# First batch of an agent-attention and gated-FFN kernel: loads and conversions reordered ahead of the first up product, and one cast placed behind an output copy

## The chip, the cores and the metric

The kernel runs on one core of a Trainium2 chip. The metric is the device time of one execution in microseconds (us), lower is better; runs are given by their median. The engines are named as in the profile: PE (TensorE matmuls), PEld (its weight loads), DVE (VectorE), ACT (ScalarE), POOL (GpSimd) and SP (SyncE, which issues most DMAs).

## What is computed

```python
# per batch b of 4; N = 12480 tokens, C = 128, 49 agents
def sm(a, b):
    s = scale * (a @ b.transpose(0, 2, 1)); e = np.exp(s - s.max(-1, keepdims=True))
    return e / (e.sum(-1, keepdims=True) + 1e-09)
agent_v = sm(agents, k) @ v          # over all keys of the batch
x = sm(q, agents) @ agent_v          # each query token
h = x @ w_in                         # 128 -> 2048
out = (h * sigmoid(1.702 * h)) @ w_out   # 2048 -> 128
```

Weights come as 64-bit floats and are converted on DVE.

## The kernel before, in words

The agents' values of a batch are folded into `w_in`, so that the query softmax feeds an up product of 49 rows with 2048 columns directly (`wh`, `wl` are high and low part of that folded weight). Work runs in **gaps**, one per 128 columns of the hidden layer (`f`, 16 of them) of a group of 960 query tokens (`n`, 52 groups), plus one more gap per group. A gap issues the jobs that a table `at` puts there, an up product with its two activations on ACT (`up`), a high part (`high`: a DMA cast for even `f` and for 1 and 9, else a cast on ACT), a low part on DVE (`low`, three gaps later) and two half down products (`down`, six gaps later). In the last gap of a group `store` copies the two output banks `po[0]` (ACT) and `po[1]` (DVE) to `o`; the next group's first down product writes the same two banks. Within the gaps each engine runs the instructions in the order in which the code writes them.

Ahead of the gaps stands a start phase for batch 0, whose order on each engine a scheduler makes. Its steps:

- 13 key blocks `kt0` land, `first_key_scores` multiplies each with the agents on PE, ACT copies the scores to `score`, DVE keeps a running maximum (`running_max`, L277).
- `key_max` (L285 to L302) reduces it to `max_b`; `key_shift` (L317) subtracts it and `key_exp` (L321) takes the exponentials.
- 13 value blocks `vt0` land in tiles that later hold `wh` and `wl`; 104 products (L657) sum them into `acc_ps`. Value blocks 8 to 12 reuse the tiles of blocks 0 to 5.
- `load_words` loads a quarter of `w_in` or `w_out` (512 KB); `to_float32` converts it with eight DVE instructions (L123 to L135), for `up_weights` into `w_in_sb`, for `down_weights` into `wo_h` and `wo_l`. The words share three buffers.
- `weights_0`, `weights_1` and `weights_parts` turn `acc_ps` into `avT` and fold it into `w_in_sb` (L383), which gives `wh` (ACT, L386) and `wl` (DVE, L387).

Of the conversions only the first of `w_in` stands before the values; the others come behind them, in this code:

Of the kernel before, what the change touches and what calls it, by code (L numbers as in the profile page):

```python
# [8 lines left out]
F32 = mybir.dt.float32  # L9
# [10 lines left out]
KB = 8  # L20
# [10 lines left out]
P_AT = 8  # L31
K_AT = (4, 10, 13)
V_AT = (6, 10)
FIRST_WORDS = 1
FIRST_UP = 2
BY_DMA = (1, 9)
EPS = 1e-09

# [2 lines left out]
def kernel(  # L41
# [273 lines left out]
    def key_shift(g, sub):  # L315
        sc = score[:TB, g * KB : (g + 1) * KB, :]
        sub(out=sc, in0=sc, in1=max_b[:TB].unsqueeze(1).broadcast_to([TB, KB, A]), op=ALU.subtract)  # L317

    def key_exp(g, n):
        sc = score[:TB, g * KB : (g + n) * KB, :]  # L320
        nc.scalar.activation(out=sc, in_=sc, func=AF.Exp, scale=scale)  # L321
# [35 lines left out]
    def weights_0(acc, w):  # L357
# [2 lines left out]
        nc.vector.tensor_add(out=zc, in0=z[0], in1=z[1])  # L360
        w["acc"], w["zc"] = acc, zc

    def weights_1(w):
        ps = two_banks()[:, 0]
        parts = [w["acc"][:, c, i * C : (i + 1) * C] for c in range(2) for i in range(2)]
        for i, part in enumerate(parts):
            nc.tensor.matmul(out=ps[:, 0:P], lhsT=part, rhs=sel, start=(i == 0), stop=(i == len(parts) - 1))
        nc.tensor.matmul(out=ps[:, P : 2 * P], lhsT=w["zc"], rhs=sel, start=True, stop=True)
        rz = work.tile([P, P], F32, name="rz", bufs=1)
        nc.vector.tensor_scalar_add(out=rz, in0=ps[:, P : 2 * P], scalar1=EPS)  # L370
        nc.vector.reciprocal(out=rz, in_=rz)
        avT = work.tile([P, P], F32, name="avT", bufs=1)
        nc.vector.tensor_mul(out=avT, in0=ps[:, 0:P], in1=rz)
        w["avT"] = avT

    def weights_parts(b, w, c):
        if c == 0:
            wts[b] = wpool.tile([P, F], F32R, name="wh"), wpool.tile([P, F], F32R, name="wl")
        wh, wl = wts[b]
        pw = two_banks()  # L380
        for i in range(2):
            s = slice((c + i) * 512, (c + i + 1) * 512)
            nc.tensor.matmul(out=pw[:, i], lhsT=w["avT"], rhs=w_in_sb[:, s], start=True, stop=True)  # L383
        for i in range(2):
            s = slice((c + i) * 512, (c + i + 1) * 512)
            nc.scalar.copy(out=wh[:, s], in_=pw[:, i])  # L386
            nc.vector.tensor_sub(out=wl[:, s], in0=pw[:, i], in1=wh[:, s].bitcast(F32))  # L387

# [166 lines left out]
    def do_query_load(n):  # L555
        if n < B * NG:
            qts[n] = query_load(*divmod(n, NG))
# [56 lines left out]
    def first_keys():  # L614
        tags = [("g", G_BUFS), ("gh", GH_BUFS), ("gl", GL_BUFS)]
        tiles = []
        for tag, bufs in tags:
            tiles += [gpool.tile([P, KB, TB], F32, name="kt0", tag=tag, bufs=bufs) for _ in range(bufs)]
        return tiles[:NKG]

    for g, t in enumerate(first_keys()):
        nc.sync.dma_start(out=t, in_=kT[0, :, g * KB : (g + 1) * KB, :])
        kts[0, g] = t
    do_query_load(0)
    words_in = []
    for g in range(NKG):
        if g % 2 == 0:
            vt0 = wpool.tile([P, 2, KB, C + 1], F32, name="vt0", tag=("wh", "wl")[g // 2 % 2])
            nc.gpsimd.memset(vt0[:, :, :, C :], 1.0)
        vts[0, g] = vt0[:, g % 2]  # L630
        nc.sync.dma_start(out=vt0[:TB, g % 2, :, 0:C], in_=v[0, :, g * KB : (g + 1) * KB, :])
        if g == FIRST_WORDS:
            words_in.append(load_words(w_in, 0))
    words = []
    for i in range(NF // 4):
        if i:
            words_in.append(load_words(w_in, i))
        words.append(load_words(w_out, i))
    for g in range(NKG):
        first_key_scores(g, kts.pop((0, g)))  # L640
    for i in range(4):
        do_query_split(0, i)
    key_max()
    banks[0] = score_banks()
    scores_whole(0, q_parts[0], banks[0][0])
    do_query_load(1)
    do_query_shift(0)
    do_query_exp(0)
    do_query_sums(0)
    do_query_softmax(0)  # L650
    acc_ps = ps_o.tile([P, 512], F32, name="po0")
    for g in range(NKG):
        key_shift(g, nc.vector.tensor_tensor if g == 0 else nc.gpsimd.tensor_tensor)
        key_exp(g, 1)
        vt = vts.pop((0, g))
        for j in range(KB):
            nc.tensor.matmul(  # L657
                out=acc_ps[:A, : C + 1],
                lhsT=score[:TB, g * KB + j, :],
                rhs=vt[:TB, j, :],  # L660
                start=(g == 0 and j == 0),
                stop=(g == NKG - 1 and j == KB - 1),
            )
        if g == FIRST_UP:
            up_weights(0, words_in[0])
        if g == 6:
            do_query_pairs(0)
    accs[0] = work.tile([P, 2, 2 * C + 1], F32, name="acc")
    nc.gpsimd.memset(accs[0], 0.0)
    nc.vector.tensor_copy(out=accs[0][:A, 0, 0:C], in_=acc_ps[:A, 0:C])  # L670
    nc.vector.tensor_copy(out=accs[0][:A, 0, 2 * C :], in_=acc_ps[:A, C : C + 1])
    w0 = {}
    weights_0(accs.pop(0), w0)
    weights_1(w0)
    up_weights(1, words_in[1])
    weights_parts(0, w0, 0)
    down_weights(0, words[0])


    steps = B * NG * NF  # L680
# [37 lines left out]
        take(t + P_AT, 1)  # L718
        put(t + P_AT, lambda m=m: do_query_pairs(m))

    put(0, lambda: up_weights(2, words_in[2]))
    put(1, lambda: down_weights(1, words[1]))
    put(2, lambda: up_weights(3, words_in[3]))
    take(3, 1)
    put(3, lambda: weights_parts(0, w0, 2))
    put(5, lambda: down_weights(2, words[2]))
    put(7, lambda: down_weights(3, words[3]))
    for b in range(B - 1):
        begin = gap_of(b * NG * NF)
        end = gap_of((b + 1) * NG * NF)  # L730
# [47 lines left out]
    po = {}  # L778

    late = []  # L780

    def do_high(u):
        gh[u] = high(u % NF, g[u])

    def do_up(u):
        n, f = divmod(u, NF)
        g[u] = up(f, wts[n // NG], pairs[n])
        if by_dma(f):
            late.append(u)
        else:  # L790
            do_high(u)
        if f == NF - 1:
            pairs.pop(n)

# [14 lines left out]
    def gap(t):  # L809
        n, k = divmod(t - LAG, GAPS)  # L810
        final = n == B * NG - 1
        if t < LAG:
            u = t
        elif final:
            u = n * NF + LAG + k
        elif k == 1:
            u = None
        else:
            u = n * NF + LAG + max(k - 1, 0)
        before, late[:] = list(late), []  # L820
        rest()
        for job in at.pop(t, ()):
            job()
        if u is not None:
            if u < steps:
                do_up(u)
                rest()
            do_low(u - 3)
        if t >= LAG:
            do_downs(n, k)  # L830
        for u in before:
            do_high(u)

    def do_downs(n, k):
        if k == 0:
# [53 lines left out]
```

## Time and profile before

| | |
|---|---|
| runs | 2028.25, 2022.54, 2024.57 us, median 2024.57 |
| profiled execution | 2026.61 us, its span 2024.8 us |
| PE busy | 1953.1 us, 96% of the span |
| DVE, ACT, POOL busy | 77%, 69%, 15% |
| mean granted clock of TensorE | 0.986 |

The 1.8 us between span and time lie outside the profiled instructions. A busy PE is not one at its peak: the ends of matmuls are modelled, and neighbours overlap.

### The profile page before, as it was taken

Reading aid. Unit: us, or ns where it says so; the run is one execution under the profiler, and the core shown is the slowest. Engines: PE = TensorE matmul, PEld = TensorE weight load, DVE = VectorE, ACT = ScalarE, POOL = GpSimd, SP = SyncE. Lnnn points to the kernel's source line nnn. Section 1 sums busy time; section 2 is a strip of 40 time slices with the busy share of each in tenths; the row PEclk is TensorE's granted clock in tenths of the full one; section 3 lists DMA queues with packets and bytes.
Section 4 is the critical chain, followed back from the end, with each engine's and each line's share of the span. In section 5 each row is a group of like instructions: output and inputs, shape, how many; then the busy total and the mean of one; then the engine's idle time right before and its main releaser. Section 6 shows DMA issues by size and latency. Waiting matters only on the chain.

```text
span 2024.8 us, 59521 instructions
## 1 busy us (share of the span) xinstructions
PE 1953.1 (96%) x25158; PEld 1771.6 (87%) x25158; DVE 1553.4 (77%) x2025; ACT 1404.0 (69%) x2407; POOL 303.4 (15%) x642
## 2 busy tenths in 40 slices
PE   8789999999999999999999999999999999999998
PEld 8578998988988989998988889888898998999987
DVE  5687878887878888887867887888886766676765
ACT  3267777767667667677667677777776787777775
POOL 3011111111111111111111111111111111111111
PEclk9689999999999999999999999999999999999999
DMA  9555565666545665656554566566654544545453
GB/s 256 153 166 178 195 186 183 192 192 195 175 160 191 194 191 184 196 181 182 186 167 167 190 203 190 183 186 186 186 172 139 176 170 172 174 171 180 167 177 137
DMA packets 124336, 365.98 MB, mean 181 GB/s; under 512 B 12572, under 2 KB 38492, under 8 KB 124068
## 3 DMA queue, kind: packets, MB, share of 16 engines
q0 software_dynamic: 74880, 255.62, 36.6%
q1 hardware_dynamic: 49188, 106.55, 19.5%
q8 instruction: 197, 3.23, 0.7%
q14 instruction: 71, 0.58, 0.1%
HBM read 80.97 MB, written 25.56 MB: 53 GB/s over the span
## 4 chain that ended last, share of the span: by engine, by line
PE 80%; ACT 8%; DVE 4%; issue 4%; DMA 3%; SPq 0%; POOL 0%; ACTq 0%; DVEq 0%; POOLq 0%
PE po L192 46%; PE ph L192 24%; PE ps_m L192 7%; ACT g L480 3%; DMA gh<-g 2%; ACT L480 1%; DVE gl L496 1%; ACT L406 1%; PE ph L261 1%; ACT o L526 1%; PE ps_m L383 1%; ACT score L321 1%; DVE rest L173 0%; PE po L657 0%; PE po L518 0%
## 5 line engine op out<-in xcount | busy, mean ns | idle before, releaser
L480 ACT ACTIVATE g<-ph 128x480 f32<-128x480 f32 x1664 | 850.8, 570 | 474.3 <-PE ph L192 469.4
L496 DVE TENSOR_TENSOR gl<-g,gh 128x960 fp32r<-128x960 f32 x832 | 944.5, 1152 | 239.8 <-DMA gh<-g 177.8
L192 PE MATMUL po<-gh,wo_h 64*128 64x480 f32 x3300 | 799.0, 383 | 23.1 <-ACT o L526 18.1
L192 PE MATMUL po<-gl,wo_h 64*128 64x480 f32 x3300 | 789.0, 378 | 0.0
L192 PE MATMUL po<-gh,wo_l 64*128 64x480 f32 x3300 | 787.3, 377 | 0.0
L489 POOL DMA_DIRECT2D gh<-g x520 | 275.2, 529 | 1677.6 <-PE ph L192 799.5
L192 PEld LDWEIGHTS po<-gh,wo_h 64*128 64x128 f32 x3300 | 460.2, 185 | 62.7 <-ACT o L526 36.7
L192 PEld LDWEIGHTS po<-gh,wo_l 64*128 64x128 f32 x3300 | 461.9, 185 | 19.7
L192 PEld LDWEIGHTS po<-gl,wo_h 64*128 64x128 f32 x3300 | 463.2, 186 | 17.0
L192 PE MATMUL ph<-q_hi,wh 49*128 49x480 f32 x1664 | 431.8, 406 | 9.1 <-ACT g L480 8.3
L192 PE MATMUL ph<-q_lo,wh 49*128 49x480 f32 x1664 | 405.6, 380 | 0.0
L192 PE MATMUL ph<-q_hi,wl 49*128 49x480 f32 x1664 | 402.1, 379 | 0.0
L491 ACT CAST gh<-g 128x960 fp32r<-128x960 f32 x312 | 311.5, 998 | 9.9
L192 PEld LDWEIGHTS ph<-q_hi,wh 49*128 49x128 f32 x1664 | 237.5, 186 | 44.6 <-ACT g L480 29.1
L192 PEld LDWEIGHTS ph<-q_hi,wl 49*128 49x128 f32 x1664 | 237.6, 186 | 9.9 <-DVE wl L387 0.2
L192 PEld LDWEIGHTS ph<-q_lo,wh 49*128 49x128 f32 x1664 | 237.3, 188 | 6.1
L192 PE MATMUL ps_m<-ag_part,rest 64*128 64x49 bf16 x4320 | 143.2, 182 | 9.4 <-DVE rest L173 8.3
L192 PEld LDWEIGHTS <-rest 64*128 64x128 bf16 x4320 | 121.9, 94 | 11.9 <-DVE rest L173 11.3
L173 DVE TENSOR_TENSOR rest<-rest 128x488 bf16<-128x488 f32 (+1 forms) x182 | 131.0, 720 | 0.0
L192 PE MATMUL ps_m<-ag_part,qt 64*128 64x49 bf16 x2448 | 85.5, 184 | 0.2 <-DVE acc L354 0.2
L192 PEld LDWEIGHTS <-qt 64*128 64x128 bf16 x2448 | 68.7, 94 | 18.4 <-issue 14.2
L192 PEld LDWEIGHTS <-kt 64*128 64x128 bf16 x1872 | 50.2, 94 | 20.7 <-issue 20.1
(102 smaller groups left out, 1279.7 us busy)
## 6 DMA issues: line engine op xcount, KB each, us to landing
gh<-g POOLq DMA_DIRECT2D x520, 480.0 KB, 3.2
kt<-kT SPq DMA_DIRECT2D x52, 480.0 KB, 4.1
qt<-qT SPq DMA_DIRECT2D x52, 480.0 KB, 4.6
vt<-v SPq DMA_DIRECT2D x52, 480.0 KB, 5.3
outT<-o SPq DMA_DIRECT2D x104, 240.0 KB, 2.4
words<-w_in SPq DMA_DIRECT2D x4, 512.0 KB, 5.9
words<-w_out SPq DMA_DIRECT2D x4, 512.0 KB, 6.4
ag_sb<-agT SPq DMA_DIRECT2D x1, 98.0 KB, 2.0
```

What stands on the lines that cost most here:

```text
L173: nc.vector.tensor_sub(out=halves(r)[1][:, s], in0=r[:, s], in1=halves(r)[0][:, s])
L192: ins = nc.tensor.matmul(tile_position=(c * H, 0), **kw)
L261: nc.tensor.matmul(out=ps[:TB, j * 2 * A : (j + 1) * 2 * A], lhsT=kt[:, c * KB // 2 + j, :], rhs=ag_sb[:, 0:2, :].rearrange("p b a -> p (b ...
L321: nc.scalar.activation(out=sc, in_=sc, func=AF.Exp, scale=scale)
L383: nc.tensor.matmul(out=pw[:, i], lhsT=w["avT"], rhs=w_in_sb[:, s], start=True, stop=True)
L406: nc.scalar.activation(out=e, in_=e, func=AF.Exp, scale=scale)
L480: nc.scalar.activation(out=g[:, c, :], in_=ph[c][:, :CH], func=AF.Gelu_apprx_sigmoid)
L489: nc.gpsimd.dma_start(out=gh, in_=g)
L491: nc.scalar.copy(out=gh, in_=g)
L496: nc.vector.tensor_sub(out=gl, in0=g, in1=gh.bitcast(F32))
L526: nc.scalar.copy(out=o, in_=po[c][:, :CH])
```

## The change

Loads: each quarter of `w_in` is loaded behind three or four key blocks and converted among the key blocks (`WORDS_AT`); the quarters of `w_out` are loaded among the value blocks, two of them are converted while the values are summed (`WORDS_DONE`), the other two in gaps 4 and 6. Value blocks land two token rows at a time (rows of 1024 B in place of 512 B), with a column of ones on either side of the pair, so that the sums come out in columns 0 and 129. All 13 key shifts run on DVE, ahead of the query softmax; POOL did 12 of them. `first_weights` normalizes before it transposes (one product and 49 rows in place of five products). `weights_parts` writes each folded product directly before its casts. In the gaps, ACT's cast of the high part is written behind `do_downs`, and so behind `store`'s copy.

```diff
+WORDS_DONE = 2
+WORDS_AT = {0: (3, 6, 9, 12), 1: (2, 5, 8, 11)}
...
+    def first_weights(acc_ps):
+        av = work.tile([P, C], F32, name="av0", tag="zc", bufs=1)
+        nc.vector.tensor_copy(out=av[:A], in_=acc_ps[:A, 1 : C + 1])
+        z = work.tile([P, 2], F32, name="z0", bufs=1)
+        nc.vector.tensor_copy(out=z[:A, 0:1], in_=acc_ps[:A, 0:1])
+        nc.vector.tensor_scalar(
+            out=z[:A, 1:2], in0=acc_ps[:A, C + 1 : C + 2], scalar1=z[:A, 0:1], scalar2=EPS, op0=ALU.add, op1=ALU.add
+        )
+        nc.vector.reciprocal(out=z[:A, 0:1], in_=z[:A, 1:2])
+        nc.vector.tensor_scalar_mul(out=av[:A], in0=av[:A], scalar1=z[:A, 0:1])
+        ps = two_banks()[:, 0]
+        nc.tensor.matmul(out=ps[:, 0:P], lhsT=av[:A], rhs=sel[:A], start=True, stop=True)
+        avT = work.tile([P, P], F32, name="avT", bufs=1)
+        nc.vector.tensor_copy(out=avT, in_=ps[:, 0:P])
+        return {"avT": avT}
...
         for i in range(2):
             s = slice((c + i) * 512, (c + i + 1) * 512)
             nc.tensor.matmul(out=pw[:, i], lhsT=w["avT"], rhs=w_in_sb[:, s], start=True, stop=True)
-        for i in range(2):
-            s = slice((c + i) * 512, (c + i + 1) * 512)
             nc.scalar.copy(out=wh[:, s], in_=pw[:, i])
...
     for g, t in enumerate(first_keys()):
         nc.sync.dma_start(out=t, in_=kT[0, :, g * KB : (g + 1) * KB, :])
         kts[0, g] = t
+        if g in WORDS_AT[0]:
+            words_in.append(load_words(w_in, len(words_in)))
+        first_key_scores(g, kts.pop((0, g)))
+        if g in WORDS_AT[0]:
+            i = len(words_in) - 1
+            up_weights(i, words_in[i])
...
+        nc.sync.dma_start(
+            out=vt0[:TB, g % 2, :, 1 : 2 * C + 1],
+            in_=v[0, :, g * KB : (g + 1) * KB, :].rearrange("t (i j) c -> t i (j c)", j=2),
+        )
+        if g in WORDS_AT[1]:
+            words_out.append(load_words(w_out, len(words_out)))
...
+    for g in range(NKG):
+        key_shift(g, nc.vector.tensor_tensor)
+        key_exp(g, 1)
     do_query_shift(0)
...
     for g in range(NKG):
-        key_shift(g, nc.vector.tensor_tensor if g == 0 else nc.gpsimd.tensor_tensor)
-        key_exp(g, 1)
         vt = vts.pop((0, g))
         for j in range(KB):
+            i, c = divmod(j, 2)
             nc.tensor.matmul(
-                out=acc_ps[:A, : C + 1],
+                out=acc_ps[:A, c : c + C + 1],
                 lhsT=score[:TB, g * KB + j, :],
-                rhs=vt[:TB, j, :],
+                rhs=vt[:TB, i, c * (C + 1) : (c + 1) * (C + 1)],
...
-        if g == FIRST_UP:
-            up_weights(0, words_in[0])
-        if g == 6:
+        if g < WORDS_DONE:
+            down_weights(g, words_out[g])
+        if g == 8:
             do_query_pairs(0)
...
-    weights_0(accs.pop(0), w0)
-    weights_1(w0)
-    up_weights(1, words_in[1])
+    w0 = first_weights(acc_ps)
     weights_parts(0, w0, 0)
-    down_weights(0, words[0])
...
-    put(0, lambda: up_weights(2, words_in[2]))
-    put(1, lambda: down_weights(1, words[1]))
-    put(2, lambda: up_weights(3, words_in[3]))
-    take(3, 1)
-    put(3, lambda: weights_parts(0, w0, 2))
-    put(5, lambda: down_weights(2, words[2]))
-    put(7, lambda: down_weights(3, words[3]))
+    take(2, 1)
+    put(2, lambda: weights_parts(0, w0, 2))
+    for i in range(WORDS_DONE, NF // 4):
+        put(2 * i, lambda i=i: down_weights(i, words_out[i]))
...
         g[u] = up(f, wts[n // NG], pairs[n])
-        if by_dma(f):
-            late.append(u)
-        else:
-            do_high(u)
+        (late if by_dma(f) else soon).append(u)
...
-        for u in before:
+        for u in before + soon:
             do_high(u)
+        soon.clear()
```

The first place is DVE at the end of the key blocks, up to the maximum's reduction (`mx`); `tmp`, `m_...` and `w_in_sb` belong to a conversion, `rest` to the query's split. Before:

```order
L277 TENSOR_TENSOR run_max<-score,run_max 120x392 x11
L171 TENSOR_TENSOR rest<-qt 128x488
L171 TENSOR_TENSOR rest<-qt 128x480
L277 TENSOR_TENSOR run_max<-score,run_max 120x392
L173 TENSOR_TENSOR rest<-rest 128x488
L173 TENSOR_TENSOR rest<-rest 128x480
L285 TENSOR_REDUCE mx<-run_max 120x49
```

And now, from the last conversion of `w_in` on:

```order
L123 TENSOR_SCALAR tmp<-words 128x512
L277 TENSOR_TENSOR run_max<-score,run_max 120x392
L124 TENSOR_SCALAR tmp<-tmp 128x512
L130 TENSOR_SCALAR m_356<-words 128x512
L125 TENSOR_SCALAR tmp<-tmp 128x512
L131 TENSOR_SCALAR tmp<-words 128x512
L126 SCALAR_TENSOR_TENSOR tmp<-words,tmp 128x512
L132 SCALAR_TENSOR_TENSOR m_356<-m_356,tmp 128x512
L171 TENSOR_TENSOR rest<-qt 128x488
L135 SCALAR_TENSOR_TENSOR w_in_sb<-m_356,tmp 128x512
L173 TENSOR_TENSOR rest<-rest 128x488
L171 TENSOR_TENSOR rest<-qt 128x480
```

All four conversions of `w_in` now stand in front of `mx`, the last seven instructions of the fourth behind the last running maximum.

The second place is DVE around the end of the values (`po_434`, `po_473` hold their sums). Before, from the wait for the second quarter of `w_in`:

```order
L131 TENSOR_SCALAR tmp<-words 128x512
L670 COPY acc<-po_434 49x128
L671 COPY acc<-po_434 49x1
L126 SCALAR_TENSOR_TENSOR tmp<-words,tmp 128x512
L360 TENSOR_TENSOR zc<-acc 128x128
L132 SCALAR_TENSOR_TENSOR m_631<-m_631,tmp 128x512
L370 TENSOR_SCALAR rz<-ps_m 128x128
L135 SCALAR_TENSOR_TENSOR m_631<-m_631,tmp 128x512
L371 RECIPROCAL rz<-rz 128x128
L145 TENSOR_TENSOR wo_l<-m_631,wo_h 128x512
L373 TENSOR_TENSOR avT<-ps_m,rz 128x128
```

And now:

```order
L171 TENSOR_TENSOR rest<-qt 128x488
L365 COPY av_651<-po_473 49x128
L367 COPY z_653<-po_473 49x1
L368 TENSOR_SCALAR z_653<-po_473,z_653 49x1
L371 RECIPROCAL z_653<-z_653 49x1
L372 TENSOR_SCALAR av_651<-av_651,z_653 49x128
L376 COPY avT<-ps_m 128x128
L401 TENSOR_TENSOR wl<-ps_m,wh 128x512 x4
L173 TENSOR_TENSOR rest<-rest 128x488
L510 TENSOR_TENSOR gl<-g,gh 128x960
```

No conversion stands between the sums and the four casts of `wl` any more; the two that are left follow behind this piece.

The third place is ACT around a group's output copy (`o`), where `g<-ph` are the activations. Before:

```order
L480 ACTIVATE g<-ph 128x480 x4
L491 CAST gh<-g 128x960
L526 COPY o<-po_852 128x480
L480 ACTIVATE g<-ph 128x480 x4
L491 CAST gh<-g 128x960
```

And now:

```order
L494 ACTIVATE g<-ph 128x480 x4
L540 COPY o<-po_865 128x480
L505 CAST gh<-g 128x960
L494 ACTIVATE g<-ph 128x480 x4
L505 CAST gh<-g 128x960
```

The cast and the copy have changed places; nothing else of ACT's order in the gaps has.

## Rows read from the trace of the kernel before

**Rows 1.** The page: busy us by engine, share of the span, instructions.

```profile
PE 1953.1 (96%) x25158; PEld 1771.6 (87%) x25158; DVE 1553.4 (77%) x2025; ACT 1404.0 (69%) x2407; POOL 303.4 (15%) x642
```

**Rows 2.** Waits: engine, line, waited for; us in total, times, longest.

```profile
PEld po L192 <- ACT o L526: 36.7, 46, 1.5
...
PE po L192 <- ACT o L526: 18.1, 46, 1.1
...
PEld po L192 <- DVE o L528: 6.1, 11, 1.6
```

**Rows 3.** Timeline of ACT at one store: start, duration, instruction.

```profile
1888.46 1.03 ACT L480 ACTIVATE g<-ph 128x480 f32<-128x480 f32 x2 [0.94 <-PE ph L192]
1889.53 1.00 ACT L491 CAST gh<-g 128x960 fp32r<-128x960 f32 x1
1890.43 0.55 ACT L526 COPY o<-po 128x480 f32<-128x480 f32 x1
```

**Rows 4.** Timelines of DVE and of PE at that store.

```profile
1889.29 0.66 DVE L528 COPY o<-po 128x480 f32<-128x480 f32 x1 [0.47 <-PE po L192]
...
1889.95 0.45 PE L192 MATMUL ph<-q_lo,wh 49*128 49x480 f32 x2
1890.17 0.45 PE L192 MATMUL ph<-q_hi,wl 49*128 49x480 f32 x2
1891.03 0.48 PE L192 MATMUL po<-gh,wo_h 64*128 64x480 f32 x2 [0.42 <-ACT o L526]
```

**Rows 5.** Timeline of DVE, end of the key blocks.

```profile
28.97 0.57 DVE L277 TENSOR_TENSOR run_max<-score,run_max 120x392 f32<-120x392 f32 x1 [1.11 <-ACT score L270]
29.46 1.23 DVE L171 TENSOR_TENSOR rest<-qt 128x488 f32<-128x488 f32 x2
...
32.30 0.80 DVE L285 TENSOR_REDUCE mx<-run_max 120x49 f32<-120x392 f32 x1
```

**Rows 6.** Timelines of POOL and DVE: shifts and conversions.

```profile
35.01 13.84 POOL L317 TENSOR_TENSOR score<-score,max_b 120x392 f32<-120x392 f32 x12 [30.73 <-DVE max_b L302]
...
35.37 1.17 DVE L123 TENSOR_SCALAR tmp<-words 128x512 uint32<-128x512 uint32 x1
...
60.92 0.43 DVE L123 TENSOR_SCALAR tmp<-words 128x512 uint32<-128x512 uint32 x1 [8.38 <-DMA words<-w_in]
...
62.61 0.68 DVE L132 SCALAR_TENSOR_TENSOR m<-m,tmp 128x512 f32<-128x512 uint32 x1
63.21 0.68 DVE L126 SCALAR_TENSOR_TENSOR tmp<-words,tmp 128x512 uint32<-128x512 uint32 x1
```

**Rows 7.** Timeline of PE, from the values to the first up product.

```profile
37.30 13.43 PE L657 MATMUL po<-vt,score 120*49 120x129 f32 x112 [0.23 <-ACT score L321]
...
51.05 10.83 PE L657 MATMUL po<-vt,score 120*49 120x129 f32 x96
...
71.51 3.78 PE L383 MATMUL ps_m<-w_in_sb,avT 128*128 128x512 f32 x4 [2.58 <-DVE avT L373]
76.01 0.77 PE L192 MATMUL ph<-q_hi,wh 49*128 49x480 f32 x2 [0.72 <-ACT wh L386]
```

**Rows 8.** Timeline of DVE, from `avT`'s first copy to the first later keys.

```profile
66.09 0.28 DVE L670 COPY acc<-po 49x128 f32<-49x128 f32 x1
...
92.91 0.69 DVE L387 TENSOR_TENSOR wl<-ps_m,wh 128x512 fp32r<-128x512 f32 x1 [0.65 <-ACT wh L386]
...
113.77 0.69 DVE L173 TENSOR_TENSOR rest<-rest 128x480 bf16<-128x480 f32 x1
```

**Rows 9.** Timeline of ACT: first cast of `wh`, table load.

```profile
75.37 0.58 ACT L386 CAST wh<-ps_m 128x512 fp32r<-128x512 f32 x1 [4.87 <-PE ps_m L383]
...
77.31 1.28 ACT L480 ACT_TABLE_LOAD   x1
```

**Rows 10.** Windows: length, busy by engine, PEclk (granted clock), DMA share, GB/s.

```profile
10.00:18.00 8.00, 8.00 (x70) 8.00 (x70) 2.27 (x4) 2.88 (x9) 0.00 (x0) 1.00 1.03 410
...
32.00:36.00 4.00, 1.84 (x29) 1.53 (x30) 2.91 (x7) 0.00 (x0) 0.99 (x1) 0.53 1.15 189
```

More of the change, by code (lines that the diff above doesn't have):

```diff
@@ L33 @@
 V_AT = (6, 10)
-FIRST_WORDS = 1
-FIRST_UP = 2
+WORDS_DONE = 2
+WORDS_AT = {0: (3, 6, 9, 12), 1: (2, 5, 8, 11)}
 BY_DMA = (1, 9)
@@ L619, in first_keys @@
         return tiles[:NKG]
+    words_in = []
+    words_out = []
     for g, t in enumerate(first_keys()):
@@ L623 @@
         kts[0, g] = t
+        if g in WORDS_AT[0]:
[4 more added lines that the diff above has]
+            up_weights(i, words_in[i])
     do_query_load(0)
-    words_in = []
     for g in range(NKG):
         if g % 2 == 0:
-            vt0 = wpool.tile([P, 2, KB, C + 1], F32, name="vt0", tag=("wh", "wl")[g // 2 % 2])
-            nc.gpsimd.memset(vt0[:, :, :, C :], 1.0)
+            vt0 = wpool.tile([P, 2, KB // 2, 2 * C + 2], F32, name="vt0", tag=("wh", "wl")[g // 2 % 2])
+            nc.gpsimd.memset(vt0[:, :, :, 0:1], 1.0)
+            nc.gpsimd.memset(vt0[:, :, :, 2 * C + 1 :], 1.0)
         vts[0, g] = vt0[:, g % 2]
[L631 to L640, printed above, removed]
+        nc.sync.dma_start(
[4 more added lines that the diff above has]
+            words_out.append(load_words(w_out, len(words_out)))
+    do_query_load(1)
     for i in range(4):
@@ L645 @@
     scores_whole(0, q_parts[0], banks[0][0])
-    do_query_load(1)
+    acc_ps = ps_o.tile([P, 512], F32, name="po0")
+    for g in range(NKG):
+        key_shift(g, nc.vector.tensor_tensor)
+        key_exp(g, 1)
     do_query_shift(0)
@@ L650 @@
     do_query_softmax(0)
-    acc_ps = ps_o.tile([P, 512], F32, name="po0")
     for g in range(NKG):
-        key_shift(g, nc.vector.tensor_tensor if g == 0 else nc.gpsimd.tensor_tensor)
-        key_exp(g, 1)
         vt = vts.pop((0, g))
         for j in range(KB):
+            i, c = divmod(j, 2)
             nc.tensor.matmul(
-                out=acc_ps[:A, : C + 1],
+                out=acc_ps[:A, c : c + C + 1],
                 lhsT=score[:TB, g * KB + j, :],
-                rhs=vt[:TB, j, :],
+                rhs=vt[:TB, i, c * (C + 1) : (c + 1) * (C + 1)],
                 start=(g == 0 and j == 0),
                 stop=(g == NKG - 1 and j == KB - 1),
+                skip_group_check=True,
             )
-        if g == FIRST_UP:
-            up_weights(0, words_in[0])
-        if g == 6:
+        if g < WORDS_DONE:
+            down_weights(g, words_out[g])
+        if g == 8:
             do_query_pairs(0)
[L668 to L672, printed above, removed]
-    weights_0(accs.pop(0), w0)
-    weights_1(w0)
-    up_weights(1, words_in[1])
+    w0 = first_weights(acc_ps)
     weights_parts(0, w0, 0)
-    down_weights(0, words[0])
     steps = B * NG * NF
@@ L780 @@
     late = []
+    soon = []
     def do_high(u):
```

## The prediction

> **What bounds the kernel now.** I read the page first. PE is busy 96% of the span, DVE 77%, ACT 69% [rows 1]: outside the start, an edit pays only where PE waits. The list of waits comes next. In the gaps one pair stands out: the first down product of a group waits for ACT's copy of the old sums, 46 of 51 times, for 18.1 us on PE and 36.7 us on its weight loads; for DVE's copy of the other bank it waits 11 times [rows 2]. The timelines of one store show why. ACT ends the two activations at 1889.49, casts for 1.00 us, and begins the copy only at 1890.43, although DVE's copy of the other bank could start at 1889.29 [rows 3, 4]. PE's pairs of matmuls start 0.22 us apart, so after the last up pair at 1890.17 the down product would start at 1890.39; it starts at 1891.03, just behind the copy's end at 1890.98 [rows 4]. That is some 0.6 us lost, of which the row shows 0.42 as idle, since the end of a matmul is drawn later than its neighbour's start.
>
> The second place is the start. Up to the last key PE sets the pace and DVE idles 1.11 us in each 1.68 us block [rows 5]. From 37.30 to 61.88 PE sums values nearly without a break, and the first up product starts only at 76.01 [rows 7]. DVE is why: at 60.92 it has idled 8.38 us for the second quarter of `w_in` [rows 6], converts, and takes the finished sums only at 66.09, 4.2 us after their end; conversions then stand among everything up to 113.77, where the first split of later keys comes [rows 8].
>
> **Step 1, copy ahead of cast.** The instructions and their times stay; two change places. The copy would start at 1889.53 and end at 1890.08, before PE needs it at 1890.39, so this store's loss goes whole. From the totals: 18.1 us over 46 waits is 0.39 us of drawn idle; the pipelining adds 0.16 (here 0.6 lost against 0.42 drawn), so 0.55 us each. In the 11 stores where DVE's copy ends last I count nothing, for DVE's order doesn't change. That leaves 35 x 0.55 = 19 us; a few where DVE's copy ends between the two make it 18.5. Bounds: 46 x 0.55 = 25 if DVE's copies also come earlier, 0 if another wait takes over. What is late next: the cast ends 0.55 us later, and who waits is the low part on DVE, three gaps later. The next activations don't move, since cast and copy take the same sum in either order.
>
> **Step 2, conversions of `w_in` among the keys.** Five instructions of one start within 1.69 us (60.92 to 62.61), three more take 0.60 us each [rows 6]: 1.7 + 1.8 = 3.5 us, four times 14.0. A running maximum occupies DVE 0.49 us (28.97 to 29.46) of each 1.68 us block [rows 5], so eleven blocks leave 11 x 1.19 = 13.1 us. The order puts single instructions between maxima that are not ready early on; following it by hand, DVE loses some 2.2 us so, and uses 10.9. The query's first halves, 1.2 us, lay in that idle time too. So 14.0 + 1.2 - 10.9 = 4.3 us come behind the last maximum, less 0.6 for a split that now stands behind `mx`: **`mx` moves from 32.30 to about 36.0**, and everything on PE from there with it, 3.7 us. The price hangs on the duration of 0.43 us. With POOL shifting beside it, the same instruction took 1.17 us [rows 6]; POOL has nothing to do among the keys now, so I take 0.43. By 1.17, 32 instructions would cost up to 24 us more.
>
> Loads: 13 key blocks of 128 x 960 floats (6.39 MB) and 2.10 MB of words at 410 GB/s [rows 10] are 20.7 us, begun near 3, so all are in by 24; PE multiplies the last block behind 28.97 [rows 5]. Hidden. The fourth words wait on SP until the first conversion has freed a buffer, near 17; the query and all values are queued behind, and start no earlier than the keys let them.
>
> **Step 3, values.** PE takes 10.83 us for the last six blocks, 1.8 each [rows 7]. Thirteen shifts on DVE at 0.49 (a maximum has the same shape) feed it faster than POOL's 13.84 / 12 = 1.15 us did [rows 6], and neither is on the path. Two rows at a time: rows of 512 B landed at 189 GB/s, those of 3840 B at 410 [rows 10]. Rows of 1024 B lie between. At 189 the values and the words of `w_out` need 33.8 + 5.1 us from 25 on, to 64, and PE comes to the last block at 63.5: 0 to 2 us lost. At 300 or more all is hidden, so the edit gives nothing by itself; I take 0. The Trainium skill (DMA: Bandwidth & Descriptors, section Specifications) names 512 B as the smallest transfer at line rate; by that rule the old rows were at line rate already, the edit would land nothing sooner, and the sum would lose the 0 to 2 us; the trace does not agree, with 189 against 410 GB/s. Two conversions of `w_out` (2 x 4.2 us) fall into the time in which DVE waited 8.38 us. Values end at 61.88 + 3.7 = 65.6.
>
> **Step 4, the shorter way.** DVE now takes the sums at once: five small instructions at some 0.2 us, 1.1; one product, at most 0.6; a copy, 0.28: `avT` at 67.6. A folded product is 3.78 / 2 = 1.9 us [rows 7], its cast 0.58 [rows 9]: the first up product starts at 70.1, 5.9 us earlier. Four up matmuls, 0.8; second product, 1.9; cast, 0.6; table load, 1.28 [rows 9]; four activations, 2.06 [rows 3]: 76.8. Cast and subtraction of the other half, twice, with the 0.65 us wait between [rows 8]: 2.6, so `wl` is complete at 79.4. Before it was at 92.91 + 0.69 = 93.60, since two conversions stood before it. From there to 113.77 DVE had 20.2 us of work and short waits [rows 8]; now the same two conversions and the same low parts stand there, and one split more (0.6). So that split starts at 79.4 + 20.8 = 100.2 in place of 113.77: **13.6 us**. Bounds: 9 (values 2 us late, DVE's waits for low parts longer by 2.5), 17 (products at full clock, 0.9 us each, and a shorter chain).
>
> **Sum.** 18.5 + 13.6 = 32 us. Against the profiled 2026.6 that is 1994.5; the profiled run stood 2.0 us above the median, so **1993** on the runs' scale.
>
> **Rivals.**
> - *Start only*: DVE's copies, or another wait of PE, take the place of ACT's. For it: the 11 stores, and DVE's copy lies behind a low part in each group with key work. Against it: in the shown store DVE is done at 1889.95, 0.44 before the need. 2024.6 - 13.6 = 2011, with part of the gain 2004 to 2011.
> - *Stores only*: the start gives nothing back, by slow conversions (1.17 us) or late values. 2024.6 - 18.5 = 2006; with the whole 24 us, 10 us worse than no gain, 2016.
> - *Cool PE*: PE idles 3.7 us longer between the last key and `mx`, and already before the clock was granted at 0.53 in the stretch behind that pause [rows 10]. If the products of the values stayed at 1.2 GHz (level 0.5) all along, their 24.6 us would grow by up to 23, and the start lose 9: 2016. Against it: in the trace the values ran at 1.8 us a block soon after the pause [rows 7]. The Trainium skill (TensorE: Matmul & The Clock Gate, section What's actually happening) calls the throttled state the default and says that activity releases it; by that rule the longer pause costs no more than the first one did, and the trace agrees so far.
> - *No change*: both fall away, 2024.
> - *Slower*: ACT reaches the copy before the last down product has ended, waits there instead of casting, and the next activations, and PE's next up product, come up to 0.9 us late: 51 x 0.9 = 46 against 13.6, at worst 2057; it decides from 13.6 / 51 = 0.27 us a store. Against it: the sums were ready at 1889.29, ACT free at 1889.53 [rows 3, 4].
>
> **How the numbers follow.** Forecast 0.60, its own range 1984 to 2000; start only 0.16; stores only 0.12; cool PE 0.03; no change 0.05; slower 0.04. The range 1984 to 2009 holds the forecast, most of the first two rivals, and leaves out some 2 in 10. The measurement tells 0.3%, 6 us, from no change. The first four cases are all faster: 0.91; same 0.05; slower 0.04.
>
> **What would show it.** Right: waits of PE for ACT's copy nearly gone, those for DVE's left; `mx` near 36; values' end near 65.6; first up near 70; the split of keys near 100. Wrong: conversions over 0.5 us an instruction among the keys; a clock of 0.5 beyond the first few us of values; PE waiting for activations or low parts behind each store; the last value block landing after 63.

## The result, and the profile after

The changed kernel takes 1997.6 us (median; 1995.88 to 1998.25), the kernel before 2025.1 beside it: a ratio of 0.9862, 95% interval 0.9845 to 0.9879, 27.5 us faster. The forecast was 1993. Its profiled execution took 1997.63 us, with a span of 1995.9.

In the list of waits (engine, line, waited for; us in total, times, longest) PE's wait for ACT's copy, 18.1 us in [rows 2], is gone; one of 0.5 us is left on the weight loads, and DVE's copy is now the one PE waits for:

```profile
PEld po L192 <- DVE o L542: 12.5, 19, 2.0
...
PE po L192 <- DVE o L542: 4.9, 5, 1.6
PEld po L192 <- ACT o L540: 0.5, 1, 0.5
```

ACT's timeline at the store that [rows 3] show has the copy directly behind the activations:

```profile
1862.71 1.03 ACT L494 ACTIVATE g<-ph 128x480 f32<-128x480 f32 x2 [0.94 <-PE ph L192]
1863.63 0.57 ACT L540 COPY o<-po 128x480 f32<-128x480 f32 x1
1864.07 1.02 ACT L505 CAST gh<-g 128x960 fp32r<-128x960 f32 x1
```

PE's timeline there: from the last up pair to the next group's first down product it is 0.22 us, against 0.86 in [rows 4].

```profile
1864.39 0.44 PE L192 MATMUL ph<-q_hi,wl 49*128 49x480 f32 x2
1864.61 0.45 PE L192 MATMUL po<-gh,wo_h 64*128 64x480 f32 x2
...
1867.30 0.42 PE L192 MATMUL ph<-q_hi,wh 49*128 49x480 f32 x2
```

In the kernel before, the up pair that answers to the last of these rows stands here on PE:

```profile
1893.82 0.41 PE L192 MATMUL ph<-q_hi,wh 49*128 49x480 f32 x2
```

From up pair to up pair it was 1893.82 - 1890.17 = 3.65 us, and is 1867.30 - 1864.39 = 2.91: 0.74 saved, 0.64 of it ahead of the down product and the rest in the pairs behind, which followed each other 0.33 and 0.21 us apart after the stall, and 0.22 apart without it.

The start. DVE's timeline around `mx`, predicted for 36.0, and from the finished sums to the first split of later keys (predicted 100.2):

```profile
30.32 0.42 DVE L124 TENSOR_SCALAR tmp<-tmp 128x512 int32<-128x512 int32 x1
...
35.19 0.81 DVE L285 TENSOR_REDUCE mx<-run_max 120x49 f32<-120x392 f32 x1
...
71.64 0.28 DVE L365 COPY av<-po 49x128 f32<-49x128 f32 x1 [1.93 <-PE po L677]
...
73.38 0.29 DVE L376 COPY avT<-ps_m 128x128 f32<-128x128 f32 x1 [0.64 <-PE ps_m L374]
...
87.16 0.69 DVE L401 TENSOR_TENSOR wl<-ps_m,wh 128x512 fp32r<-128x512 f32 x1 [2.78 <-ACT wh L400]
...
108.66 0.70 DVE L173 TENSOR_TENSOR rest<-rest 128x480 bf16<-128x480 f32 x1
```

`mx` and the way from the sums to `avT` are near the forecast, the end of the values is not. PE's timeline shows why: it waits for the last blocks to land.

```profile
58.83 1.94 PE L677 MATMUL po<-vt,score 120*49 120x129 f32 x16 [0.47 <-DMA vt<-v]
61.18 1.94 PE L677 MATMUL po<-vt,score 120*49 120x129 f32 x16 [0.41 <-DMA vt<-v]
63.70 1.94 PE L677 MATMUL po<-vt,score 120*49 120x129 f32 x16 [0.57 <-DMA vt<-v]
68.20 3.41 PE L677 MATMUL po<-vt,score 120*49 120x129 f32 x16 [2.56 <-DMA vt<-v]
...
75.95 0.77 PE L192 MATMUL ph<-q_hi,wh 49*128 49x480 f32 x2 [1.01 <-ACT wh L400]
```

These four waits are 4.0 us. In the last of them the granted clock also fell, from 1.00 to 0.50 at 67.8 (the lower level, 1.2 GHz), after PE had idled for 2.2 us, and the last block's 16 products took 3.41 us in place of 1.94. DVE takes the sums at 71.64, where 65.6 had been predicted, and the first up product starts at 75.95, no earlier than before (76.01, [rows 7]). The split of later keys comes at 108.66 in place of 113.77: 5.1 us, not 13.6. Windows of the stretch in which the values land, and of one farther on (length, busy by engine, granted clock, DMA share, GB/s):

```profile
26.00:66.00 40.00, 30.56 (x283) 28.86 (x282) 28.78 (x63) 10.26 (x23) 0.72 (x6) 0.87 1.05 220
28.00:36.00 8.00, 1.44 (x14) 1.28 (x13) 7.97 (x17) 0.77 (x3) 0.00 (x0) 0.85 1.04 221
...
102.00:121.00 19.00, 17.34 (x244) 15.78 (x244) 16.40 (x25) 15.06 (x26) 2.86 (x7) 1.00 0.59 192
```

The last of these windows in the kernel before:

```profile
102.00:121.00 19.00, 12.16 (x161) 9.72 (x158) 15.99 (x25) 10.09 (x16) 1.88 (x4) 0.73 0.35 112
```

The DMA engines are busy all through and move 220 GB/s, little over the 189 that [rows 10] show for rows of 512 B. In the last window the granted clock is 1.00, with PE busy for 17.34 of 19 us; in the kernel before it was 0.73, with PE busy for 12.16, that is, part of the time at the lower level. PE has more work by then: the last down product of the first group starts at 138.58 and 7.9 us earlier than before, 2.8 more than the split.

Last, the group of the folded products in the list by line (busy, mean ns; idle before, what ended it):

```profile
L399 PE MATMUL ps_m<-w_in_sb,avT 128*128 128x512 f32 x32 | 20.9, 740 | 10.2 <-DVE wl L401 9.9 <-DVE avT L376 0.4
```

These 9.9 us are a wait that the kernel before did not have in any batch, and that the prediction did not name.

### The profile page after: what moved, and what is told of

Its sections match the earlier page's. It is cut to its first block, busy times and chain, and to the rows that moved or that the text cites. A ratio compares the mean times of both kernels' runs of the same rounds, so it can differ in the third digit from the quotient of the medians.

```text
span 1995.9 us, 59375 instructions
## 1 busy us (share of the span) xinstructions
PE 1937.5 (97%) x25150; PEld 1811.9 (91%) x25150; DVE 1551.2 (78%) x2037; ACT 1399.3 (70%) x2407; POOL 289.4 (15%) x636
## 4 chain that ended last, share of the span: by engine, by line
PE 84%; DVE 5%; ACT 5%; DMA 3%; issue 2%; SPq 0%; DVEq 0%; POOLq 0%; ACTq 0%
PE po L192 47%; PE ph L192 26%; PE ps_m L192 8%; DMA gh<-g 2%; DVE gl L510 1%; ACT g L494 1%; ACT L494 1%; PE ps_m L399 1%; ACT L420 1%; DMA vt<-v 1%; PE ph L261 1%; ACT score L321 1%; DVE rest L173 1%; PE po L532 0%; DVE score L317 0%
## 5 line engine op out<-in xcount | busy, mean ns | idle before, releaser
L192 PE MATMUL po<-gh,wo_h 64*128 64x480 f32 x3300 | 820.1, 381 | 6.9 <-DVE o L542 4.9
L192 PE MATMUL po<-gl,wo_h 64*128 64x480 f32 x3300 | 812.1, 378 | 0.1
L192 PE MATMUL po<-gh,wo_l 64*128 64x480 f32 x3300 | 807.2, 376 | 0.0
L192 PEld LDWEIGHTS po<-gh,wo_h 64*128 64x128 f32 x3300 | 482.1, 184 | 24.3 <-DVE o L542 12.5
L192 PEld LDWEIGHTS po<-gl,wo_h 64*128 64x128 f32 x3300 | 484.1, 186 | 9.3 <-DVE gl L510 0.9
L192 PEld LDWEIGHTS po<-gh,wo_l 64*128 64x128 f32 x3300 | 482.8, 184 | 10.1
L192 PEld LDWEIGHTS ph<-q_hi,wh 49*128 49x128 f32 x1664 | 243.5, 185 | 35.4 <-ACT g L494 23.4
L192 PEld LDWEIGHTS ph<-q_hi,wl 49*128 49x128 f32 x1664 | 243.3, 185 | 7.7 <-issue 1.5
L192 PEld LDWEIGHTS ph<-q_lo,wh 49*128 49x128 f32 x1664 | 243.3, 188 | 3.2
L171 DVE TENSOR_TENSOR rest<-qt 128x488 f32<-128x488 f32 x104 | 68.5, 659 | 9.3 <-DMA qt<-qT 9.3
## 6 DMA issues: line engine op xcount, KB each, us to landing
words<-w_in SPq DMA_DIRECT2D x4, 512.0 KB, 10.5
```

The source lines that it names most:

```text
L171: nc.vector.tensor_sub(out=r[:, s], in0=t[:, s], in1=halves(t)[0][:, s])
L192: ins = nc.tensor.matmul(tile_position=(c * H, 0), **kw)
```

## The experiments

Twelve kernels ran, each beside the kernel before.

| run | median us | ratio to before, 95% interval |
|---|---|---|
| the change | 1997.6 | 0.9862 (0.9845 to 0.9879) |
| e1 copy only | 1999.96 | 0.9875 (0.9855 to 0.9895) |
| e2 start only | 2021.33 | 0.9981 (0.9972 to 0.9991) |
| e3 values, rows of 4096 B | 1994.9 | 0.9851 (0.9835 to 0.9867) |
| e4 values, rows of 512 B | 2000.53 | 0.9874 (0.9857 to 0.9891) |
| e5 4096 B, tokens together | 1995.19 | 0.9859 (0.9839 to 0.988) |
| e6 1024 B, tokens together | 1997.81 | 0.9868 (0.9848 to 0.9887) |
| e7 products paired again | 1994.7 | 0.9854 (0.983 to 0.9878) |
| e8 words behind values | 1995.88 | 0.9856 (0.9833 to 0.9879) |
| e9 as e5, 128 partitions | 1991.97 | 0.9845 (0.9826 to 0.9865) |
| e10 e8 and paired products | 1986.08 | 0.9817 (0.9804 to 0.9831) |
| e11 e10, one conversion later | 1985.98 | 0.9819 (0.9806 to 0.9832) |
| e12 e11, 128 partitions | 1985.66 | 0.9827 (0.9813 to 0.984) |

Single executions of one kernel differ by up to 10 us, so a difference under some 4 us is read from the traces, not from two medians.

**The two halves of the change.** e1 is the kernel before with this one edit of the gaps:

```diff
-        if by_dma(f):
-            late.append(u)
-        else:
-            do_high(u)
+        (late if by_dma(f) else soon).append(u)
...
-        for u in before:
+        for u in before + soon:
             do_high(u)
+        soon.clear()
```

> The kernel before with one edit of the change alone: ACT's cast of the high part stands behind the copy of the output. Theory: the gain of this edit is a matter of the gaps alone and adds to that of the start. The change gained 27.5 us in the median; its last down product of the first group ends 7.9 us earlier, so the stores and the rest should hold about 20 us: 2005 us (2002 to 2008), PE's waits for ACT's copy nearly gone, the start as before. Rival: the stores gave only what the prediction's rival 'Start only' left them, and the start more: 2011 to 2018.

Measured: 25.1 us by the medians, more than the theory expected. In its list of waits ACT's copy is gone and the waits for DVE's are as in the change:

```profile
PEld po L192 <- DVE o L528: 13.6, 19, 1.9
PE po L192 <- DVE o L528: 5.7, 7, 1.5
PEld po L192 <- ACT o L526: 0.5, 1, 0.5
```

e2 is the changed kernel with that edit undone.

> The changed kernel with the cast ahead of the copy again, so that only the edits of the start remain. Theory: they give about 8 us, as the end of the first group's last down product shows: 2017 us (2014 to 2020), and the waits for ACT's copy are back at some 46 of 51 stores. Rival: the 13.6 us of the prediction are there but hidden by something that the cast's place brings: 2011.

Measured: 3.8 us by the medians, less than either theory. PE's wait for ACT's copy is back:

```profile
PEld po L192 <- ACT o L540: 39.8, 48, 1.6
PE po L192 <- ACT o L540: 20.2, 46, 1.2
```

25.1 and 3.8 make 28.9, against 27.5 for both: within what is uncertain they add. The gain is nearly all from the copy. In e2's trace the start does better than its 3.8 us: the last down product of the first group starts 10.5 us earlier than in the kernel before. Part of that is given back later. From the start of a group's last down product to that of the next, groups 11, 24 and 37 (counted from 0) take 40.89, 40.84 and 40.90 us in e2 and took 39.10, 39.12 and 39.14 before: 1.8, 1.7 and 1.8, together 5.3 us. These are the groups in which later batches fold their weights. So an edit of the start costs there, and e7 undoes it.

**The folded products.** e7:

```diff
         for i in range(2):
             s = slice((c + i) * 512, (c + i + 1) * 512)
             nc.tensor.matmul(out=pw[:, i], lhsT=w["avT"], rhs=w_in_sb[:, s], start=True, stop=True)
+        for i in range(2):
+            s = slice((c + i) * 512, (c + i + 1) * 512)
             nc.scalar.copy(out=wh[:, s], in_=pw[:, i])
```

> The changed kernel with the two folded products again ahead of their casts, as before the change. Theory: writing each product directly before its casts makes PE wait 1.4 us for DVE's subtraction in two gaps of each of the other three batches, which shows as 1.7 to 1.8 us in each of groups 11, 24 and 37 of the run without the cast's move: without it the time is 4 to 5.5 us lower, 1992 to 1994, if the first batch loses at most 1 us by its later first up product. Rival: PE finds other waits in those groups, or the first batch gives it back: 1996 to 1999.

By the medians it gained 2.9 us, between what its theory and its rival had said, and the intervals overlap. The traces decide. In the change PE's timeline of group 11 shows two products with a wait between:

```profile
542.09 1.12 PE L399 MATMUL ps_m<-w_in_sb,avT 128*128 128x512 f32 x2
544.67 1.12 PE L399 MATMUL ps_m<-w_in_sb,avT 128*128 128x512 f32 x2 [1.46 <-DVE wl L401]
```

In e7 they run in one go, and the group of all folded products, in the list by line, has lost the wait:

```profile
540.27 1.99 PE L399 MATMUL ps_m<-w_in_sb,avT 128*128 128x512 f32 x4
```

```profile
L399 PE MATMUL ps_m<-w_in_sb,avT 128*128 128x512 f32 x32 | 19.5, 739 | 0.4 <-DVE avT L376 0.4
```

Both products write the one tile `pw`, each a half of it; written behind the casts, the second waits until DVE has read the first half. Groups 11, 24 and 37 take 40.32, 40.01 and 40.11 us in the change and 38.63, 38.35 and 38.43 in e7: 1.7 each, 5.0 together. In the first batch nothing was lost: `wl` is complete 14.2 us behind `avT` in the change (73.67 to 87.85) and 14.0 in e7 (73.66 to 87.67).

**The landing of the values.** e3 lands a block as whole rows of 4096 B and sums the exponentials on DVE in place of the columns of ones; e4 goes back to rows of 512 B.

```diff
# e3
-            out=vt0[:TB, g % 2, :, 1 : 2 * C + 1],
-            in_=v[0, :, g * KB : (g + 1) * KB, :].rearrange("t (i j) c -> t i (j c)", j=2),
+            out=vt0[:TB, g % 2], in_=v[0, :, g * KB : (g + 1) * KB, :]
...
# e4
+            out=vt0[:TB, g % 2, :, 0:C], in_=v[0, :, g * KB : (g + 1) * KB, :]
```

> The changed kernel with each block of values landed as rows of 4096 B, whole per partition; the column of ones falls away, and DVE adds up the exponentials (13 additions) in its place, with one small product behind the last values. Theory: the last value blocks land late in the changed kernel and cost some 6 us, so values end near 66 in place of 71.6, the keys' split of L173 comes 5 to 8 us earlier, and the time is 1990 to 1992. Rival: DVE's chain behind the values, or the half clock, sets the start anyway: values end earlier, but the split stays within 2 us of 108.7 and the time near 1997.

> The changed kernel with each block of values landed one row of 512 B at a time, as before. Theory: at the 187 GB/s that rows of 512 B had before, the 6.4 MB of values and 1 MB of words need 39 us from 26 on, near 66, some 3 to 5 us later than in the changed kernel's 35 us: values end near 75, and the time is 2001 to 2003. Rival: the landing sets nothing: 1997 to 1998. A third possibility: the two sizes share one rate when the words are queued between the values, and the landing ends at the same time in both: 1997 to 1999.

That landing sets the end of the values held: PE's last wait and the end moved with it, to 75.5 with rows of 512 B and 69.1 with rows of 4096 B, from 71.6 in the change. By the medians the times were 2.9 us above and 2.7 below the change's, in the order that the theory forecast, though the intervals overlap; e3's values ended 3 us later than it had said, and its time lies between theory and rival. PE's timeline of the last block in e4, then in e3 (the granted clock was low again, 0.57 and 0.54 in these two stretches):

```profile
72.15 3.34 PE L672 MATMUL po<-vt,score 120*49 120x129 f32 x16 [3.07 <-DMA vt<-v]
```

```profile
65.60 3.48 PE L670 MATMUL po<-vt,score 120*49 120x128 f32 x16 [2.68 <-DMA vt<-v]
```

But the size of a row explains little. In the window from 28 to 36, e4 moved 209 GB/s, the change 221, and e3, whose rows are longer than those of the keys, which land at 410 in the same trace:

```profile
28.00:36.00 8.00, 1.95 (x19) 1.78 (x17) 7.96 (x17) 0.97 (x3) 0.00 (x0) 0.92 0.98 243
10.00:18.00 8.00, 8.00 (x74) 8.00 (x74) 5.23 (x12) 2.90 (x9) 0.00 (x0) 1.00 1.02 410
```

So something else slows the values. e5 (from e3) and e6 (from the change) give a block 960 tokens that lie together in memory; keys are laid out to match:

```diff
-        "kT": k.reshape(B, TB, NJ, C).transpose(0, 3, 2, 1),
-        "v": v.reshape(B, TB, NJ, C),
+        "kT": k.reshape(B, NJ // KB, TB, KB, C).transpose(0, 4, 1, 3, 2).reshape(B, C, NJ, TB),
+        "v": v.reshape(B, NJ // KB, TB, KB, C),
```

> The run with value blocks in rows of 4096 B, with one more edit: a block now holds 960 tokens that lie together in memory, so that its 120 rows follow each other there; before, row followed row at a distance of 53,248 B (keys are laid out to match, and the sums over all tokens stay the same). With rows of 4096 B at that distance the values landed at only 240 GB/s, against 410 for keys in rows of 3840 B, so the size of a row is not what holds them. Theory: the distance of the rows holds them; now they land at 380 to 410 GB/s, all blocks are in by 48 or as soon as their buffers come free, values end at 65 to 66 without a wait of PE above 0.5 us, and the time is 2 to 4 us below that of the run with the old distance: 1991 to 1993. Rival: the tile side holds them (120 partitions, or the reading and writing that PE, ACT and DVE do meanwhile): the rate stays at 220 to 250 GB/s, values end near 69, the time near 1995.

> The changed kernel with only that edit: rows of 1024 B, two tokens each, but a block's tokens lie together in memory. Theory: distance matters and size little: over 300 GB/s, values end at 65 to 67, 1991 to 1994. Rival of the prediction (size matters): 215 GB/s as in the changed kernel, values end near 70, 1997.

This theory fell: e5 moved 247 GB/s in that window, e6 222. The distance in memory is not it. The window in e5:

```profile
28.00:36.00 8.00, 1.29 (x13) 1.16 (x11) 7.96 (x17) 0.65 (x2) 0.00 (x0) 0.85 0.97 247
```

e9 is e5 with transfers that fill all partitions:

```diff
-            out=vt0[:TB, g % 2], in_=v[0, g]
+            out=vt0[:, g % 2], in_=v.rearrange("b g t j c -> (b g t) j c")[g * TB : g * TB + P]
```

> The run with value blocks of 960 tokens that lie together, in rows of 4096 B, with each block's transfer widened from 120 rows on 120 partitions to 128 rows on 128 partitions; the 8 rows more are the next block's and nobody reads them. Neither the size of the rows nor their distance in memory explains 240 GB/s; keys (rows of 3840 B) and words (rows of 4096 B) landed at 380 to 420 GB/s, both on 128 partitions. Theory: the 120 partitions hold the values: now 380 to 410 GB/s from 26 on, blocks wait only for their buffers. Rival: what runs beside them (DVE's shifts, PE's reading of the values, the conversions) holds them: 230 to 260 GB/s as before. In both cases the time stays near 1995, within 3 us, since PE by then waits only some 2 us for values.

This edit brought the rate. The window from 28 to 36 in e9:

```profile
28.00:36.00 8.00, 1.82 (x18) 1.65 (x16) 7.96 (x17) 0.97 (x3) 0.00 (x0) 0.89 1.03 408
```

It is 408 GB/s in place of 247, with rows of the same size and distance and the same work beside them. Partitions written and rows read went from 120 to 128 together; which of the two it is, no run tells. PE waits for no value block, values end at 64.1, and the first up product starts at 67.8. The time, 1991.97 from two executions, is at the lower end of what was expected.

e8 tests the landing from the other side, by moving 1.05 MB of words behind the values:

```diff
-WORDS_AT = {0: (3, 6, 9, 12), 1: (2, 5, 8, 11)}
+WORDS_AT = {0: (3, 6, 9, 12), 1: (2, 5)}
...
     do_query_load(1)
+    while len(words_out) < NF // 4:
+        words_out.append(load_words(w_out, len(words_out)))
```

> The changed kernel with the last two quarters of w_out, 1.05 MB, loaded behind all values in place of among them. Theory: landing sets the end of the values; at some 220 GB/s the last block lands up to 4.8 us earlier, values end at 66.5 to 69, and the time is 1 to 4 us lower: 1993.5 to 1996.5; the conversions of these two quarters, in gaps 4 and 6, still find their words landed. Rival: DVE then waits for the words (over 1 us at L112's tiles) or the values' end doesn't move: 1997 or more.

Values end at 67.7, as the theory had it, although `mx` came 1.1 us later in this trace; PE's last wait for them is 0.53 us. From `mx` to the values' end it is 31.4 us here and 36.4 in the change. 1.05 MB at 220 GB/s would be 4.8 us, but the 5.0 is not that landing alone: PE's waits for blocks went from 4.0 us to 1.4; the last block, behind a short wait and at a granted clock of 1.00, took 1.94 us in place of 3.41; and the first nine blocks took 17.12 in place of 18.07, with the clock at 0.58 from 36 to 44 where the change had 0.51. PE began the last block 2.5 us earlier (65.75 against 68.20). By the median the gain of 1.7 us is not told from none; in the trace the first group's last down product starts 3.1 us earlier.

**Together.** e10 is e8 with the products paired for the later batches; e11 takes the fourth conversion of `w_in` from the keys to the values; e12 is e11 with e9's blocks, in rows of 1024 B.

```diff
# e10, in weights_parts
+        for i in range(2 if b else 0):
+            s = slice((c + i) * 512, (c + i + 1) * 512)
+            nc.tensor.matmul(out=pw[:, i], lhsT=w["avT"], rhs=w_in_sb[:, s], start=True, stop=True)
         for i in range(2):
             s = slice((c + i) * 512, (c + i + 1) * 512)
-            nc.tensor.matmul(out=pw[:, i], lhsT=w["avT"], rhs=w_in_sb[:, s], start=True, stop=True)
+            if b == 0:
+                nc.tensor.matmul(out=pw[:, i], lhsT=w["avT"], rhs=w_in_sb[:, s], start=True, stop=True)
...
# e11
-            up_weights(i, words_in[i])
+            if i < 3:
+                up_weights(i, words_in[i])
...
+        if g == 4:
+            up_weights(3, words_in[3])
...
# e12
-            out=vt0[:TB, g % 2, :, 1 : 2 * C + 1],
-            in_=v[0, :, g * KB : (g + 1) * KB, :].rearrange("t (i j) c -> t i (j c)", j=2),
+            out=vt0[:, g % 2, :, 1 : 2 * C + 1],
+            in_=v.rearrange("b g t (i j) c -> (b g t) i (j c)", j=2)[g * TB : g * TB + P],
```

> The changed kernel with two of the edits tried: the last two quarters of w_out loaded behind the values, and the two folded products ahead of their casts for the later three batches (for the first batch each directly before its casts, as in the change). Theory: the two gains are in different places and add, 2 us and 3 to 5 us: 1991 to 1993. Rival: they overlap, 1994 to 1995.

> The run with both of these edits, and the conversion of the fourth quarter of w_in moved from among the keys to among the values. Theory: the four conversions put some 4 us behind the last key's maximum; with three the maximum comes about 2 us earlier, values start and end earlier by that as long as their blocks have landed, and the time is 1 to 2 us below the run without this edit: 1989 to 1992. Rival: landing is the bound again, or the fourth conversion delays the first up products: no gain, or 1 us worse.

> The last run (words of w_out behind the values, paired products for later batches, fourth conversion among the values) with blocks of 960 tokens that lie together and transfers of 128 rows on 128 partitions, each row still two tokens of 1024 B at a time. Widening to 128 partitions took rows of 4096 B from 240 to 410 GB/s. Theory for 1024 B: the partitions held these too, so they land at 300 GB/s or more, and by their own size no longer at 215; since PE has hardly a wait for values left in the last run, the time stays within 2 us of it: 1984 to 1988. Rival: at 1024 B the size holds the rate by itself: 215 to 250 GB/s on 128 partitions too, the same time.

e10 is faster than the change: 0.9817 with an interval that ends at 0.9831, below the change's 0.9845. It came out 5 us under the lower end of what was expected; 2.5 of these lie in the kernel before, which took 2022.6 us beside it. Against that it gained 36.5 us, 9.0 more than the change. Its trace shows the two places: the first group's last down product starts 4.1 us earlier (134.44), and groups 11, 24 and 37 take 5.0 less together (38.63, 38.34 and 38.45). In e11's timeline of DVE the last maximum of the keys and `mx` now follow each other:

```profile
29.74 0.57 DVE L277 TENSOR_TENSOR run_max<-score,run_max 120x392 f32<-120x392 f32 x1 [0.37 <-ACT score L270]
30.34 0.81 DVE L285 TENSOR_REDUCE mx<-run_max 120x49 f32<-120x392 f32 x1
```

Values end at 62.7, and the first up product starts at 66.98 in place of 71.84 in e10. This earlier start of 5 us did not show in the medians of e11 and e12, which are e10's within their intervals. e11 was expected 1 to 2 us below e10, so that is a miss; e12's time lies in its 1984 to 1988. In the traces the first group's last down product starts at 134.44 in e10, 129.25 in e11 and 127.66 in e12, and from there to the last group's it is 1848.4, 1845.9 and 1851.7 us: e12 gives half of its lead back in later groups. But e10's trace is of its slowest execution, e11's of its fastest, so the traces don't decide it, and it stays open. On rates e12 gave an answer; the window from 28 to 36 in e11, then in e12:

```profile
28.00:36.00 8.00, 3.39 (x50) 3.01 (x50) 7.10 (x16) 1.46 (x5) 0.00 (x0) 0.84 1.04 224
...
28.00:36.00 8.00, 3.39 (x57) 3.01 (x56) 7.10 (x15) 1.82 (x5) 0.00 (x0) 0.79 1.09 362
```

Rows of 1024 B land at 362 GB/s on 128 partitions, against 224 in e11 on 120.

## Why the prediction was right, and where its sum was not

The time fell into its range, with the forecast 5 us too low, but its two terms, 18.5 and 13.6, were wrong in opposite directions: 25.1 and 3.8 by e1 and e2. One was 6.6 too small and the other 9.8 too large; that the sum came so near is luck. Of the signs that it named, the waits of PE and `mx` came as said; the values' end, the first up product and the split of keys came 6.0, 5.9 and 8.5 us late, and one sign of being wrong was there: the last value block landed at 68.2, after 63.

**Step 1, copy ahead of cast:** the mechanism and the count held, the size of one store was too small. Between e2 and the change 36 of 51 groups became shorter by 0.4 to 1.2 us, by 0.72 in the mean, 25.9 in sum (all 51 together by 24.2); predicted were 35 of 0.55. The term added 0.16 for pipelining to the drawn idle, where its own rows give 1891.03 - 1890.39 = 0.64 lost against 0.42 drawn, that is 0.22; and the shown store gained 0.74, since the pairs behind the stall ran slower too. For the stores where DVE's copy ends last nothing was counted, and PE still waits 4.9 us for it, 5 times.

**Step 2, conversions among the keys:** right. `mx` starts at 35.19 (36.0 predicted), an instruction takes 0.42 to 0.43 us, and the conversions did not slow down as the rival *Stores only* had it. e11 shows the price: with three conversions among the keys `mx` starts at 30.34.

**Step 3, values:** "I take 0" is the step that failed. Values were finished 6.0 us late, where the step allowed for 2 at most: 4.0 are waits for landing blocks, and 1.5 the last block at the lower clock, which the step had not counted. The landing was predicted to end at 64 at the latest, 33.8 us for the values at 189 GB/s and 5.1 for the words at 410. In fact words and values share one rate, 220, but that alone gives the same time: their 8.49 MB at 220 are 38.6 us. What the sum left out are loads that nobody waits for yet. The second query block and the next batch's first key block are issued right behind the last value block:

```profile
53.06 0.46 SPq L653 DMA_DIRECT2D vt<-v  x1
53.62 3.62 SPq L406 DMA_DIRECT2D qt<-qT  x1
```

They do not wait for it; they share the DMA engines with it. From 25.6, where the keys' rate ends, to the landing of the last value block at 68.2 the loads moved 9.38 MB. That is 0.89 more than values and words, most of the 0.98 MB of these two blocks, and 0.89 MB at 220 GB/s are 4.0 us. No run issued these two later, so this is read from the trace and not tested. The step also looked for the cause of the low rate in the size of the rows, as "rows of 1024 B lie between" 189 and 410; by e3 and e9 most of that distance belongs to the 120 partitions. What it quoted from the Trainium skill (DMA: Bandwidth & Descriptors, section Specifications), that 512 B is the smallest transfer at line rate, comes off better than the prediction gave it: on 120 partitions rows eight times as long brought 243 in place of 209 GB/s. On 128 partitions 1024 B still stayed below 4096 B, 362 against 408, and 512 B were not tried there. The shorter rows also land beside columns of ones, and no run separates this from their size.

**Step 4, the shorter way:** from the finished sums to `avT` 2.0 us, as said. To the complete `wl` 14.2 in place of 11.8. For the second half of the columns the sum counted two casts and two subtractions with a wait between, 2.6 us, and no product; from its first cast at 83.06 to the end it took 4.8, since the last product stands in that chain, behind a wait for DVE and at a granted clock of 0.50:

```profile
84.43 2.08 PE L399 MATMUL ps_m<-w_in_sb,avT 128*128 128x512 f32 x2 [1.40 <-DVE wl L401]
```

e7's order, which pairs the products, gains nothing there (14.0), since its second pair starts only at 81.21, behind the first up products. From there the split of keys comes 20.8 us later, exactly the predicted distance. Of the 8.5 us by which the split missed 100.2, the values make 6.0 and the way to `wl` 2.4. What the step left out is the same code in batches 1 to 3: written once for the first batch, `weights_parts` costs 1.7 to 1.8 us in each of the others, 5 us of the start's gain.

**The rivals:** *Stores only* came nearest: the start gave back little, by late values, one of the two reasons it named. *Cool PE* came in part: the granted clock was 0.51 from 36 to 44, against 0.81 in the kernel before, but back at 1.00 from 43.9 until 67.8 in the change, so the products of the values did not run at the lower level all along, as the rival needed. *Start only* and *Slower* fell with the missing waits for ACT's copy, and with them *No change*.

**Open:** why 120 partitions slow the loads; how much the loads queued behind the values cost; why the earlier start of e11 and e12 does not show in their medians.

## What to carry to other kernels

Price everything that is queued in a stretch at the rate of that stretch, also what would land faster alone and what is issued right behind the load that you wait for, and look at the partitions that a transfer fills before its row size. An edit of shared code that is made for one place is to be priced at every place that runs it. A copy that frees a buffer belongs ahead of work that nobody waits for, and a stall costs more than its drawn idle time.

## What the runs showed of the hardware

The window from 28 to 36 holds loads of values with a load of words among them. With the values on 120 partitions it moved 209, 221 and 243 GB/s with rows of 512, 1024 and 4096 B, with the DMA engines busy all the time (shares of 0.98 to 1.04); with the values on 128 partitions 362 with rows of 1024 B and 408 with rows of 4096 B. Widening the transfer by rows that nobody reads made it 1.65 times as fast (408 against 247). By the packets in the trace each one took longer, the words' too, which fill 128 partitions: their packets of 4096 B took 270 ns on average beside the values in the change, and 159 among the keys. Where the rows lie in memory made no difference (222 against 221 GB/s).

A wait of 2.56 us in front of the last value block left PE at the lower clock, and its 16 products took 3.41 us; behind the wait of 0.53 us in e8 the clock stayed at 1.00 and they took 1.94.
